# Linear attention into an RWKV channel mix on one core: another written-out order of the same pieces

## The chip, the core and the metric

The kernel runs on one core of one Trainium2 chip. The metric is the device time of one execution in microseconds (us); for the kernel before it is the median of three runs. The core has TensorE (PE in the profile; PEld is its weight load), VectorE (DVE), ScalarE (ACT), GpSimd (POOL) and SyncE (SP). Each works through its own list of instructions in the order in which the program gave them, and waits on semaphores for the others. POOL and SP issue DMAs here. The profile calls the queue of POOL's DMAs q0 (software_dynamic) and that of SP's DMAs q1 (hardware_dynamic); the packets of both go through the core's 16 DMA engines.

## The reference

The program computes attention without a softmax, normalizes each head by its root mean square, and feeds the result to a channel mix:

```python
kv = np.einsum('bhsd,bhse->bhde', k, v)          # q, k, v: 8 batches, 8 heads, 576 rows, 64 columns
out = np.einsum('bhsd,bhde->bhse', q, kv)
x = out / sqrt(mean(out*out, axis=-1) + 1e-6) * g_norm   # heads side by side: (8, 576, 512)

x_prev = x shifted down by one row, zeros first
xk = mu_k * x + (1 - mu_k) * x_prev
xr = mu_r * x + (1 - mu_r) * x_prev
k = relu(xk @ w_k)                               # 512 -> 1024
v = (k * k) @ w_v                                # 1024 -> 512
r = sigmoid(xr @ w_r)                            # 512 -> 512
return r * v                                     # float32
```

Inputs and output are float32; the kernel works in bfloat16 with float32 sums. The inputs are 28.3 MB of q, k and v and 5.2 MB of weights; the output is 9.4 MB.

## The kernel before

The work has two halves. The **attention** runs over 8 batches b. The **mix** runs over 9 groups g of 512 rows of all batches laid end to end, so a group needs the x of one or two batches: group 0 needs batch 0, group g batches g-1 and g, and group 8 batch 7.

Every step is a named *piece*, a function that issues a few instructions. `Plan.add` records a piece with the engines that it may run on and the pieces that it needs; `Plan.emit` (L95) goes through the string ORDER (L15) word by word and issues each piece. `@A` or `@D` behind a name puts it on ScalarE or VectorE where it may run on either. So ORDER alone sets the order on every engine and every DMA queue. The framework adds the semaphores that data and buffers need.

The pieces, by the first letters of their names (b is a batch, z a half of four heads, g a group):

- `ld.kB.z`, `ld.vB.z`, `ld.qB.z`, `ld.wk`, `ld.wr`, `ld.wv`: loads, issued on POOL (L272, L277, L292), converting to bfloat16. At most eight are in flight: each waits for the one eight before it.
- `z:512` (L478): a matmul on zeros, with no use but to keep TensorE busy. 35 of them, the last at 15.8 us.
- `kv` (L305), `kc` (copy, L182 or L184), `ks` (a split by a permutation, L311), `kd` (copy back): the 64x64 state of each head. `tq` (L390): q transposed on VectorE. `u` (L321): q times state, one PSUM tile for each half of the heads.
- `uc` (L188 on ScalarE, L190 on VectorE): a copy of u to SBUF, scaled by g. `sq` (L411, ScalarE): the square of u. Both read the same PSUM tile, and the framework lets the one that comes later in ORDER wait for the other.
- `ss` (L420, L436): sums of squares by a matmul. `rs` (L326, ScalarE): one over the root. From batch 2 on the factor comes out for each head once, into the single buffer `rsc`, and `sp` (L458) spreads it over the partitions by four DMAs on SP for each half. The next `rs` waits until both `sp` before it have landed.
- `mul` (L433, VectorE): u times the factor, that is x. `d` (L338): x minus the row before. `mk`, `mr` (L188 or L190): d times a column of mu. `xk`, `xr` (L351): the inputs of the mix.
- `k` (L510 for group 0, L534): xk @ w_k, two pieces for each PSUM tile; `relu` (L493, ScalarE); `ksq` (L521, L544, VectorE): the square. `r` (L556), `sig` (L566, ScalarE). `v` (L576), in two halves of the 1024 inner columns: `v2.3.0` is group 2, rows 384 to 511, first half.
- `out` (L589, L603, VectorE): sig times v; `out2.1` is for the rows of `v2.2.*` and `v2.3.*`. `st` (L484): the store of 128 rows, 256 KB, issued on SP.

`rs` needs another function table on ScalarE than `sig`; going from one to the other costs an ACT_TABLE_LOAD (L198). PSUM has four tiles of two banks for all of `kv`, `u`, `ss`, `k`, `r` and `v`; a piece that opens a tile waits until the readers of an earlier one are done. The buffers that matter below: three of k, v and q, three of `out` (each for two stores), three of `rs`, one `rsc`.

Of the kernel before, what the change touches and what calls it, by code (L numbers as in the profile page):

```python
# [19 lines left out]
d0.01 z:512 z:512 ks0.1 kd0.1@A z:512 u0.1.0 sq0.10 k0.000 uc0.10@A mk0.01@D xk0.01 u0.1.1 uc0.11@D sq0.11  # L20
ss0.10 k0.010 ss0.11 ld.wv0 ld.wv1 rs0.10 mul0.10 k0.110 d0.10 rs0.11 mk0.10@D xk0.10
mr0.00@A mul0.11 d0.11 mr0.10@A k0.011 relu0.01 xr0.10 mk0.11@D xk0.11 mr0.11@A k0.001 k0.100
mr0.01@D xr0.01 relu0.00 k0.111 xr0.00 relu0.11 k0.101 ld.v2.01 ksq0.01 xr0.11 relu0.10 ksq0.00
ld.k2.01 r0.0 tq1.01.1 r0.2 r0.3 sig0.1 r0.1 tq1.01.0 ksq0.10 ksq0.11 sig0.0 kv1.01
kc1.01@A ks1.01 kd1.01@A u1.01.1 uc1.11@D sq1.11 sq1.01 u1.01.0 uc1.10@D sq1.00 sq1.10 uc1.01@D
v0.1.0 v0.0.0 ss1.2 ss1.3 uc1.00@D ss1.0 v0.0.1 rs1.2 rs1.3 mul1.1 d1.1 rs1.0
ss1.1 rs1.1 mul1.0 d1.0 mk1.0@D v0.1.1 mk1.1@A v0.2.0 v0.2.1 xk1.1 mr1.1@A v0.3.0
v0.3.1 xk1.0 kv2.01 k1.4 k1.5 ld.q2.01 mr1.0@A kc2.01@A out0.0 ks2.01 kd2.01@A k1.2
tq2.01.1 relu1.2 k1.3 tq2.01.0 u2.01.1 out0.1 uc2.01@D relu1.1 k1.0 sq2.01 ld.v3.01 u2.01.0
sq2.11 sq2.00 sq2.10 uc2.11@D ld.k3.01 uc2.10@D k1.1 uc2.00@D ksq1.1 xr1.1 kv3.01 ss2  # L30
xr1.0 ld.q3.01 tq3.01.1 k1.6 k1.7 rs2 sp2.1 kc3.01@A ks3.01 r1.0 ld.q4.01 r1.1
# [19 lines left out]
v3.2.0 v3.2.1 ksq4.0 u7.01.1 mul5.0 sq7.01 ss6 mul5.1 st2.2 st2.1 rs6 uc7.01@D
sp6.0 d5.0 mr5.0@D v3.3.0 v3.3.1 ksq4.1 out3.1 r4.2 r4.3 sq7.11 v4.3.0 uc7.11@A
v4.3.1 sig4.1 u7.01.0 uc7.00@A st3.2 sq7.00 d5.1 mr5.1@A st2.0 v4.2.0 sp6.1 v4.2.1
mk5.1@D mk5.0@D v4.0.0 v4.0.1 xk5.1 xk5.0 out4.1 st4.2 xr5.0 k5.0 k5.6 st3.3
sq7.10 mul6.0 d6.0 uc7.10@A v4.1.0 ss7 mk6.0@D xk6.0 k5.1 k5.7 rs7 v4.1.1
k5.4 k5.5 relu5.3 mul6.1 relu5.0 k5.2 sp7.0 d6.1 st3.0 relu5.2 mr6.1@A xr5.1
mk6.1@D xk6.1 k6.6 mr6.0@D xr6.0 ksq5.0 k5.3 relu5.1 xr6.1 sp7.1 k6.2 ksq5.1
mul7.0 k6.3 relu6.1 k6.7 ksq6.1 relu6.3 k6.0 k6.1 r6.2 r6.3 d7.0 k6.4
k6.5 sig6.1 ksq5.3 relu6.2 ksq5.2 relu6.0 ksq6.0 ksq6.3 ksq6.2 r4.0 r4.1 v5.0.0
v5.0.1 mk7.0@D r6.0 v5.1.0 sig4.0 out4.0 r6.1 st4.0 sig6.0 v6.2.0 v6.2.1 mul7.1  # L60
v6.3.0 v6.3.1 d7.1 mr7.1@A st4.1 v6.1.0 xr7.1 mk7.1@A out6.1 st6.2 mr7.0@A xr7.0
r5.2 v6.0.0 v6.0.1 r5.3 r5.0 r5.1 xk7.0 sig5.1 sig5.0 xk7.1 v5.1.1 out5.0
st5.0 st5.1 st4.3 st6.3 k7.0 k7.6 k7.7 relu7.3 k7.2 k7.3 v6.1.1 k7.1
relu7.0 ksq7.3 v5.3.0 relu7.1 ksq7.1 v5.3.1 r8.2 out6.0 ksq7.0 k8.2 k8.3 v5.2.0
r8.3 relu8.1 st6.1 v5.2.1 ksq8.1 sig8.1 k7.4 k7.5 relu7.2 v7.1.0 ksq7.2 k8.6
k8.7 relu8.3 r7.2 r7.3 v7.2.0 v7.1.1 sig7.1 k8.0 out5.1 st5.2 ksq8.3 k8.1
r7.0 relu8.0 ksq8.0 r7.1 sig7.0 v7.3.0 k8.4 st6.0 v7.3.1 v7.0.0 v7.0.1 out7.0
st7.0 v7.2.1 out7.1 st7.3 st7.2 v8.1.00 k8.5 relu8.2 st7.1 ksq8.2 r8.0 st5.3
r8.1 sig8.0 v8.0.00 v8.1.10 v8.0.10 out8.00 st8.00 out8.10 st8.10 v8.2.00 v8.2.10 out8.20
# [575 lines left out]
```

## Time and profile before

| | |
|---|---|
| median of three runs | 208.15 us (207.28 to 208.63) |
| the profiled execution, its own time | 206.6 us |
| its span in the profile | 204.8 us |
| TensorE busy | 190.8 us, 1761 matmuls |
| VectorE busy | 136.6 us |
| ScalarE busy | 128.6 us, 10 table loads of 1.28 |
| DMA | 30.04 MB; loads (q0) 16.78 MB, spreads and stores (q1) 12.86 MB |

The times in the sections below count from the start of the span. The profile's part 2 cuts the span into 40 slices of 5.1 us and gives for each the busy share in tenths; matmuls are pipelined, so a busy TensorE is not a TensorE at its peak. In a row of the chain or the timeline the first number is the start and the second the length; in a row of the waits the numbers are the total, the count and the longest; in a row of the stretches the pairs are the engines' busy time and counts, and then come the granted clock of TensorE, the busy share of the DMA engines and GB/s.

From the trace one also sees the packets of each queue. The loads leave q0 in the order of their issue, without a pause until 96.4 us. The packets of the spreads and stores leave q1 in order as well:

| SP's DMA | issued (first, last) | packets, last end |
|---|---|---|
| sp2.1, sp2.0 | 54.05, 59.27 | 65.50 |
| st0.0, st0.2, st0.1 | 59.96, 61.04 | 67.38, 69.13, 71.91 |
| sp3.0, sp3.1 | 67.47, 72.36 | 79.73 |
| st1.3, st1.2 | 73.69, 74.07 | 81.94, 84.91 |
| sp4.1 | 82.69, 85.00 | 89.77 |
| st0.3 | 85.64 | 91.30 |
| sp4.0 | 86.32, 88.20 | 94.91 |
| st1.1, st2.3, st1.0 | 88.84, 93.46 | 95.21, 96.29, 97.84 |
| sp5.0, sp5.1 | 107.08, 112.38 | 114.14 |

### The profile page before, as it was taken

To read this page: it belongs to the slowest core of one execution; us is meant where nothing else is said; L and a number is where in the kernel's file an instruction comes from. 1 tells how busy PE (TensorE), PEld (TensorE's weight loads), DVE (VectorE), ACT (ScalarE), POOL (GpSimd) and SP (SyncE) were. 2 spreads that over 40 slices of the span, in tenths; PEclk is the share of its full clock that TensorE was granted. 3 is DMA by queue.
4 is the path that set the end of the run, shared out by engine and by line. 5 is a ranking of instruction groups with operands and counts; after the bars stand their busy time and mean duration, and the time that the engine had idled before them with its cause. 6 is when DMAs were issued, how large, how long until landed. Compare 5 with 4: busy or idle time off the path is not lost.

```text
span 204.8 us, 4262 instructions
## 1 busy us (share of the span) xinstructions
PE 190.8 (93%) x1761; PEld 94.0 (46%) x1761; DVE 136.6 (67%) x224; ACT 128.6 (63%) x171; POOL 24.5 (12%) x43
## 2 busy tenths in 40 slices
PE   7988895998899799998999999999999999999992
...
DMA  5999999999999999999003525360021051020254
GB/s 81 178 207 217 201 207 206 216 204 217 206 227 248 257 245 239 232 253 266 10 0 87 186 54 169 110 153 11 2 102 51 0 205 54 0 102 0 103 198 163
DMA packets 21015, 30.04 MB, mean 147 GB/s; under 512 B 1916, under 2 KB 14980, under 8 KB 20996
## 3 DMA queue, kind: packets, MB, share of 16 engines
q0 software_dynamic: 11808, 16.78, 46.2%
q1 hardware_dynamic: 9044, 12.86, 19.8%
...
## 4 chain that ended last, share of the span: by engine, by line
PE 61%; DVE 12%; ACT 9%; DMA 7%; SPq 5%; issue 3%; ACTq 0%; DVEq 0%
PE ps L534 20%; PE ps L576 18%; PE ps L556 13%; SPq L458 5%; DMA out_dram<-out 4%; PE ps L478 4%; DMA rs<-rsc 3%; ACT sq L411 3%; PE ps L510 3%; DVE uT L190 2%; DVE qT L390 2%; PE ps L321 2%; DVE out L589 2%; ACT rs L326 2%; PE ps L305 1%
## 5 line engine op out<-in xcount | busy, mean ns | idle before, releaser
L576 PE MATMUL ps<-w_v,sqk 128*128 128x512 bf16 (+1 forms) x296 | 67.1, 373 | 1.4 <-ACT sq L411 1.4
L534 PE MATMUL ps<-xk,w_k 128*128 128x512 bf16 (+1 forms) x288 | 59.2, 356 | 2.4 <-DVE xk L351 1.6
L493 ACT ACTIVATE relu<-ps 128x1024 bf16<-128x1024 f32 x36 | 36.1, 1024 | 30.9 <-PE ps L534 28.3
L576 PEld LDWEIGHTS <-sqk 128*128 128x128 bf16 x296 | 28.5, 98 | 33.7 <-issue 2.8
L534 PEld LDWEIGHTS <-w_k 128*128 128x128 bf16 x288 | 27.5, 98 | 29.5 <-issue 2.6
L544 DVE TENSOR_TENSOR sqk<-relu 128x1024 bf16<-128x1024 bf16 x32 | 21.4, 685 | 22.3 <-ACT relu L493 15.9
L556 PE MATMUL ps<-w_r,xr 128*128 128x512 bf16 x144 | 34.4, 379 | 0.0
L589 DVE TENSOR_TENSOR out<-ps,sig 128x1024 f32<-128x1024 f32 x16 | 19.4, 1220 | 11.2 <-PE ps L576 4.6
L566 ACT ACTIVATE sig<-ps 128x1024 bf16<-128x1024 f32 x18 | 18.2, 1025 | 10.3 <-PE ps L556 10.1
L411 ACT ACTIVATE sq<-ps 128x576 bf16<-128x576 f32 (+2 forms) x32 | 19.7, 651 | 7.5 <-DVE uT L190 4.8
L390 DVE STREAM_TRANSPOSE qT<-q 128x576 f32<-128x576 f32 (+1 forms) x18 | 20.7, 1192 | 4.3 <-DMA q<-in_q_dram 4.2
L188 ACT ACTIVATE md<-d,cols 128x576 bf16<-128x576 bf16 (+2 forms) x32 | 20.9, 720 | 0.5 <-DVE d L338 0.5
L556 PEld LDWEIGHTS <-xr 128*128 128x128 bf16 x144 | 13.6, 98 | 16.3 <-issue 0.9
L190 DVE TENSOR_SCALAR uT<-ps,cols 128x576 bf16<-128x576 f32 (+2 forms) x16 | 12.7, 815 | 10.2 <-ACT sq L411 7.0
L433 DVE TENSOR_TENSOR xT<-uT,rs 128x1152 bf16<-128x1152 bf16 (+2 forms) x18 | 12.3, 687 | 5.3 <-ACT rs L326 3.6
L351 DVE TENSOR_TENSOR xr<-md,xT 128x1152 bf16<-128x1152 bf16 (+2 forms) x18 | 12.1, 687 | 3.2 <-ACT md L188 3.1
L198 ACT ACT_TABLE_LOAD x10 | 12.8, 1283 | 0.9 <-PEq L629 0.7
L338 DVE TENSOR_TENSOR d<-xT 128x1152 bf16<-128x1152 bf16 (+2 forms) x18 | 12.4, 689 | 0.5
L190 DVE TENSOR_SCALAR md<-d,cols 128x576 bf16<-128x576 bf16 (+2 forms) x40 | 12.3, 351 | 0.5
L188 ACT ACTIVATE uT<-ps,cols 128x576 bf16<-128x576 f32 (+2 forms) x16 | 11.7, 744 | 1.1 <-PE ps L321 1.1
L351 DVE TENSOR_TENSOR xk<-md,xT 128x1152 bf16<-128x1152 bf16 (+2 forms) x18 | 12.0, 687 | 0.2
L478 PE MATMUL ps<-zero 128*128 128x512 bf16 x35 | 10.5, 448 | 1.2 <-DVE ident L219 1.2
...
## 6 DMA issues: line engine op xcount, KB each, us to landing
...
k<-in_k_dram POOLq DMA_DIRECT2D x4, 288.0 KB, 12.4
...
```

The source lines that it names most:

```text
L188: nc.scalar.mul(out=dst, in_=src, mul=col)
L190: nc.vector.tensor_scalar(out=dst, in0=src, scalar1=col, scalar2=None, op0=ALU.mult)
L351: nc.vector.tensor_tensor(out=dst[:, 2 * z:2 * z + 2, r0:r0 + w], in0=md.t[:, :, cs], in1=xT[:, :, cur], op=ALU.add)
L390: nc.vector.transpose(out=dst[part, js, :], in_=src[part, js, :])
L411: sq_ = add("sq" + name, "A", lambda _, ps=ps, sq=sq, cs=cs, w=w: nc.scalar.activation(out=get(sq)[:, :, cs], in_=ps.t[:, :, 0:w], func=AF ...
L478: nc.tensor.matmul(get(k_ps[(0, 0)])[:, 0, 0:n], zero[:, 0:128], zero[:, 0:n], start=not started, stop=not started)
L493: nc.scalar.activation(out=get(rt), in_=ps.t, func=AF.Relu)
L534: nc.tensor.matmul(get(ps)[:, fc % 2, a0:a1], w_k_sb[:, cc, 128 * fc:128 * fc + 128], xk[:, cc, x0:x0 + a1 - a0], start=(cc == 0), stop=(c ...
L544: nc.vector.tensor_mul(out=get(sqk)[:, 2 * f2:2 * f2 + 2, :], in0=rt.t, in1=rt.t)
L556: nc.tensor.matmul(get(ps)[:, ci % 2, :], xr[:, cc, n0:n0 + 128], w_r_sb[:, cc, :], start=(cc == 0), stop=(cc == NHP - 1))
L576: nc.tensor.matmul(get(ps)[:, bank, cs], sqk.t[:, fc, 128 * ci:128 * ci + 128], w_v_sb[:, fc, cs], start=(fc == 0), stop=(fc == NFC - 1))
L589: dv = add(f"out{g}.{c2}", "D", lambda _, ps=ps, sg=sg, ot=ot: nc.vector.tensor_mul(out=get(ot), in0=ps.t, in1=sg.t), deps=ms + [sg_done], ...
```

## The change

Only ORDER is changed: the sequence of its words, and the engine of some pieces that may run on two. The pieces, their instructions and their buffers are the same, and so are the 35 zero matmuls; 26 of them (`zz` and 25 more) now stand ahead of `kv0.0`, where it was 28. The new order comes out of a search over the order and the engines of all pieces, in which the readers of one PSUM tile go in turn, the copies and stores of one queue go in turn, and the loads are lengthened by both.

Of the pieces that may run on two engines, 43 are now on ScalarE and 43 on VectorE; it was 45 and 41. ScalarE goes between the tables of `rs` and `sig` so that it loads a table 12 times instead of 10. The diff, cut to the front, to batches 2 to 4 with groups 1 to 4, and to the end:

```diff
-table ld.q0.0 ld.v0.0 ld.k0.0 small ld.q0.1 ld.v0.1 ld.k0.1 ld.wk0 ld.v1.0 ld.wk1 seta
-zz z:512 z:512 z:512 z:512 z:512 z:512 z:512 z:512 z:512 z:512 z:512 z:512 z:512 z:512 z:512 z:512 z:512 z:512 z:512 z:512 z:512 z:512 z:512 z:512 z:512 z:512 z:512 kv0.0 tq0.0.1 tq0.0.0 kc0.0@A ident tr9 setb cols ld.q1.01 perm ks0.0
-tq0.1.0 tq0.1.1 ld.wr kd0.0@A z:512 u0.0.0 sq0.00 u0.0.1 sq0.01 z:512 ss0.00 rs0.00 z:512 z:512 ss0.01 uc0.00@D
-mul0.00 uc0.01@A ld.k1.1 d0.00 mk0.00@D ld.k1.0 ld.v1.1 xk0.00 rs0.01 kv0.1 mul0.01 kc0.1@A
...
-kd3.01@D tq3.01.0 relu1.0 ksq1.0 relu1.3 ksq1.3 sig1.0 r1.2 u3.01.0 tq4.01.1 sp2.0 r1.3
-v1.2.0 uc3.10@A v1.3.0 st0.0 sq3.10 st0.2 v1.0.0 sig1.1 sq3.00 uc3.00@D u3.01.1 sq3.11
-st0.1 sq3.01 v1.1.0 uc3.01@A uc3.11@A ld.k4.01 ksq1.2 v1.0.1 v1.3.1 ld.v4.01 kv4.01 mul2.1
-d2.1 mk2.1@D ss3 mul2.0 d2.0 mk2.0@D xk2.1 rs3 sp3.0 v1.1.1 v1.2.1 xk2.0
-ld.k5.01 out1.0 kc4.01@A ks4.01 ld.q7.01 tq4.01.0 kd4.01@D k2.4 k2.5 ld.k7.01 mr2.0@A mr2.1@A
-relu2.2 out1.1 xr2.0 ksq2.2 ld.v5.01 k2.2 k2.3 relu2.1 u4.01.0 sq4.00 sp3.1 uc4.10@A
-st1.3 st1.2 k2.6 sq4.10 uc4.00@D k2.7 xr2.1 ksq2.1 ld.q5.01 mul3.0 d3.0 k2.0
-relu2.3 k2.1 relu2.0 mk3.0@D ksq2.0 u4.01.1 uc4.01@A sq4.01 r2.2 r2.3 sq4.11 mul3.1
-ld.q6.01 ld.k6.01 r2.0 ksq2.3 kv5.01 uc4.11@A kc5.01@D ss4 rs4 sp4.1 sig2.1 tq5.01.1
-r2.1 sig2.0 ks5.01 kd5.01@A v2.0.0 v2.0.1 st0.3 v2.1.0 v2.1.1 mr3.0@A v2.3.0 d3.1
-mk3.1@D xk3.1 tq5.01.0 u5.01.1 sq5.01 uc5.11@A uc5.01@A sq5.11 mr3.1@A tq7.01.0 sp4.0 v2.2.0
...
-r3.0 r3.1 tq6.01.0 sig3.0 kv6.01 kv7.01 ksq3.3 kc6.01@A mk4.1@D ss5 kc7.01@D r3.2
-d4.0 mk4.0@D ks6.01 st2.3 r3.3 st1.0 kd6.01@A v3.1.0 v3.1.1 xk4.1 ks7.01 v3.0.0
-sig3.1 v3.0.1 kd7.01@D u6.01.1 xk4.0 rs5 mr4.0@A sq6.01 sq6.11 out3.0 xr4.0 sp5.0
-uc6.01@A uc6.11@D tq7.01.1 k4.6 sp5.1 k4.7 relu4.3 k4.4 k4.0 k4.1 relu4.0 k4.5
...
-v8.3.01 v8.3.11 out8.31 st8.31 v8.3.00 v8.3.10 st8.20 out8.30 st8.30
+table ld.q0.0 ld.v0.0 small ld.k0.0 ld.q0.1 ld.v0.1 ld.k0.1 seta zz z:512 z:512 z:512 z:512 z:512 z:512 z:512 z:512 z:512 z:512 z:512 z:512 z:512 z:512 z:512 z:512 z:512 z:512 z:512 z:512 z:512 z:512 z:512 z:512 z:512 kv0.0 setb
+perm tq0.0.0 ident tr9 tq0.0.1 tq0.1.1 cols kc0.0@A ks0.0 kd0.0@A z:512 u0.0.1 sq0.01
+z:512 u0.0.0 sq0.00 uc0.01@D tq0.1.0 uc0.00@A ld.wk0 z:512 z:512 ss0.00 rs0.00 kv0.1 kc0.1@A ss0.01 ks0.1
+kd0.1@A z:512 u0.1.1 rs0.01 sq0.11 ld.k1.1 ld.v1.0 ld.wk1 uc0.11@A u0.1.0 sq0.10 ld.wr z:512 z:512 ss0.11
...
+k1.7 relu1.3 ld.k3.01 u2.01.0 sq2.10 uc2.00@D k1.4 sq2.00 k1.5 u2.01.1 uc2.10@D relu1.2
+xr1.1 sq2.01 xr1.0 uc2.01@D v1.1.0 v1.0.0 sq2.11 ss2 kv3.01 uc2.11@D rs2 sp2.0
+r1.0 ksq1.3 r1.1 ksq1.2 v1.1.1 kc3.01@A tq3.01.1 tq3.01.0 ld.q4.01 ks3.01 sig1.0 sp2.1
+ld.k4.01 kd3.01@A v1.0.1 out1.0 u3.01.1 uc3.11@A sq3.11 ld.v4.01 uc3.01@A r1.2 r1.3 ld.q5.01
+v1.3.0 v1.3.1 sig1.1 kv4.01 sq3.01 u3.01.0 kc4.01@A st0.0 sq3.00 sq3.10 uc3.00@A mul2.0
+d2.0 mk2.0@D xk2.0 ld.v5.01 v1.2.0 ks4.01 kd4.01@A v1.2.1 mul2.1 uc3.10@A ss3 d2.1
+mk2.1@D rs3 sp3.0 xk2.1 mr2.1@D mr2.0@A out1.1 xr2.1 sp3.1 k2.2 k2.6 k2.7
+k2.3 relu2.1 tq4.01.0 relu2.3 tq4.01.1 ld.k5.01 ksq2.1 xr2.0 k2.0 k2.1 tq5.01.0 relu2.0
+ksq2.0 st0.2 mul3.0 ld.k6.01 st1.2 k2.4 u4.01.0 ld.q7.01 k2.5 tq5.01.1 uc4.10@A relu2.2
+r2.0 ksq2.3 r2.1 st1.0 sq4.10 r2.2 r2.3 mul3.1 v2.2.0 sq4.00 st0.3 ksq2.2
+sig2.1 v2.3.0 kv5.01 sig2.0 uc4.00@D d3.0 mk3.0@D u4.01.1 uc4.01@A kc5.01@A d3.1 v2.2.1
+ld.v6.01 v2.3.1 sq4.01 ks5.01 mk3.1@D uc4.11@A st1.1 v2.0.0 v2.0.1 kd5.01@A out2.1 u5.01.1
+xk3.0 mr3.0@D xk3.1 sq4.11 ss4 rs4 sp4.0 uc5.11@A v2.1.0 uc5.01@D v2.1.1 out2.0
+st2.0 k3.0 xr3.0 sq5.11 k3.1 sq5.01 relu3.0 k3.2 u5.01.0 mr3.1@D uc5.00@A k3.3
+sq5.00 xr3.1 ld.q6.01 k3.4 k3.5 r3.0 r3.1 mul4.0 d4.0 mk4.0@D ksq3.0 sq5.10
+uc5.10@A relu3.2 ksq3.2 sig3.0 ld.v7.01 xk4.0 sp4.1 mul4.1 k3.6 k3.7 relu3.3 d4.1
+mk4.1@D relu3.1 r3.2 r3.3 xk4.1 sig3.1 st2.3 kv6.01 ss5 mr4.0@D kc6.01@D k4.0
+k4.1 k4.6 rs5 sp5.0 k4.7 sp5.1 ksq3.1 relu4.0 ld.k7.01 tq6.01.0 tq6.01.1 ks6.01
...
+st7.3 r8.3 st8.10 v8.0.00 v8.2.00 sig8.1 v8.0.10 st7.1 out8.00 v8.2.10 out8.20 st8.20
+st8.00 v8.3.00 v8.3.01 v8.3.11 out8.31 st8.31 v8.3.10 out8.30 st8.30
```

More of the change, by code (lines that the diff above doesn't have):

```diff
@@ L20 @@
[L20 to L31, printed above, removed]
@@ L38 @@
-st1.3 st1.2 k2.6 sq4.10 uc4.00@D k2.7 xr2.1 ksq2.1 ld.q5.01 mul3.0 d3.0 k2.0
-relu2.3 k2.1 relu2.0 mk3.0@D ksq2.0 u4.01.1 uc4.01@A sq4.01 r2.2 r2.3 sq4.11 mul3.1
-ld.q6.01 ld.k6.01 r2.0 ksq2.3 kv5.01 uc4.11@A kc5.01@D ss4 rs4 sp4.1 sig2.1 tq5.01.1
-r2.1 sig2.0 ks5.01 kd5.01@A v2.0.0 v2.0.1 st0.3 v2.1.0 v2.1.1 mr3.0@A v2.3.0 d3.1
-mk3.1@D xk3.1 tq5.01.0 u5.01.1 sq5.01 uc5.11@A uc5.01@A sq5.11 mr3.1@A tq7.01.0 sp4.0 v2.2.0
-v2.3.1 out2.0 xk3.0 v2.2.1 out2.1 k3.4 k3.5 mul4.1 xr3.0 xr3.1 u5.01.0 tq6.01.1
@@ L44 @@
-relu3.2 ld.v7.01 st1.1 uc5.00@A mul4.0 k3.2 k3.3 relu3.1 ksq3.1 d4.1 mr4.1@D xr4.1
-sq5.00 k3.6 k3.7 sq5.10 ksq3.2 uc5.10@A ld.v6.01 k3.0 k3.1 relu3.0 ksq3.0 relu3.3
-r3.0 r3.1 tq6.01.0 sig3.0 kv6.01 kv7.01 ksq3.3 kc6.01@A mk4.1@D ss5 kc7.01@D r3.2
-d4.0 mk4.0@D ks6.01 st2.3 r3.3 st1.0 kd6.01@A v3.1.0 v3.1.1 xk4.1 ks7.01 v3.0.0
-sig3.1 v3.0.1 kd7.01@D u6.01.1 xk4.0 rs5 mr4.0@A sq6.01 sq6.11 out3.0 xr4.0 sp5.0
-uc6.01@A uc6.11@D tq7.01.1 k4.6 sp5.1 k4.7 relu4.3 k4.4 k4.0 k4.1 relu4.0 k4.5
-u6.01.0 relu4.2 k4.2 k4.3 sq6.00 ksq4.3 uc6.00@D uc6.10@D ksq4.2 st3.1 sq6.10 relu4.1
@@ L51 @@
[L51 to L69, printed above, removed]
-v8.3.01 v8.3.11 out8.31 st8.31 v8.3.00 v8.3.10 st8.20 out8.30 st8.30
+table ld.q0.0 ld.v0.0 small ld.k0.0 ld.q0.1 ld.v0.1 ld.k0.1 seta zz z:512 z:512 z:512 z:512 z:512 z:512 z:512 z:512 z:512 z:512 z:512 z:512 z:512 z:512 z:512 z:512 z:512 z:512 z:512 z:512 z:512 z:512 z:512 z:512 z:512 kv0.0 setb
@@ new lines @@
+perm tq0.0.0 ident tr9 tq0.0.1 tq0.1.1 cols kc0.0@A ks0.0 kd0.0@A z:512 u0.0.1 sq0.01
+z:512 u0.0.0 sq0.00 uc0.01@D tq0.1.0 uc0.00@A ld.wk0 z:512 z:512 ss0.00 rs0.00 kv0.1 kc0.1@A ss0.01 ks0.1
+kd0.1@A z:512 u0.1.1 rs0.01 sq0.11 ld.k1.1 ld.v1.0 ld.wk1 uc0.11@A u0.1.0 sq0.10 ld.wr z:512 z:512 ss0.11
+ld.v1.1 rs0.11 mul0.00 ld.q1.01 d0.00 mr0.00@D mk0.00@D z:512 z:512 ss0.10 ld.k1.0 xk0.00 k0.010 rs0.10
+xr0.00 ld.wv0 k0.000 mul0.01 d0.01 mk0.01@D xk0.01 k0.110 mr0.01@D xr0.01 uc0.10@A mul0.10
+d0.10 mk0.10@D xk0.10 k0.100 k0.001 relu0.00 ld.wv1 k0.011 relu0.01 mul0.11 d0.11 mk0.11@D
@@ new lines @@
+xk0.11 k0.101 relu0.10 mr0.10@D xr0.10 ksq0.00 r0.0 r0.1 sig0.0 k0.111 relu0.11 mr0.11@D
+xr0.11 r0.2 r0.3 tq1.01.0 tq1.01.1 sig0.1 ksq0.11 ksq0.10 ksq0.01 ld.k2.01 kv1.01 kc1.01@A
+ks1.01 kd1.01@A u1.01.1 sq1.11 uc1.11@D ld.v2.01 sq1.01 uc1.01@D u1.01.0 sq1.10 v0.0.0 uc1.10@D
+sq1.00 ss1.0 rs1.0 v0.0.1 ss1.1 ld.q2.01 uc1.00@D v0.1.0 rs1.1 ld.v3.01 ld.q3.01 mul1.0
+d1.0 ss1.3 rs1.3 ss1.2 rs1.2 mul1.1 d1.1 mk1.0@A v0.2.0 mk1.1@D v0.2.1 xk1.0
+xk1.1 v0.3.0 v0.3.1 out0.1 mr1.0@A kv2.01 kc2.01@A v0.1.1 ks2.01 k1.2 out0.0 k1.3
@@ new lines @@
+tq2.01.0 mr1.1@A relu1.1 k1.0 st0.1 tq2.01.1 ksq1.1 kd2.01@A k1.1 relu1.0 ksq1.0 k1.6
+k1.7 relu1.3 ld.k3.01 u2.01.0 sq2.10 uc2.00@D k1.4 sq2.00 k1.5 u2.01.1 uc2.10@D relu1.2
[3 more added lines that the diff above has]
+v1.3.0 v1.3.1 sig1.1 kv4.01 sq3.01 u3.01.0 kc4.01@A st0.0 sq3.00 sq3.10 uc3.00@A mul2.0
@@ new lines @@
+kd6.01@A tq7.01.1 relu4.3 v3.2.0 st1.3 ksq3.3 u6.01.0 sq6.10 sq6.00 uc6.00@A st2.1 v3.3.0
+v3.3.1 mr4.1@D uc6.10@D v3.2.1 xr4.1 u6.01.1 uc6.01@A uc6.11@A sq6.01 mul5.0 d5.0 mr5.0@D
+v3.1.0 v3.1.1 out3.1 v3.0.0 k4.2 ksq4.0 sq6.11 k4.3 relu4.1 k4.4 mul5.1 d5.1
+mk5.1@D xr4.0 kv7.01 kc7.01@D ksq4.1 ss6 rs6 k4.5 sp6.0 tq7.01.0 ks7.01 v3.0.1
+r4.2 out3.0 st3.1 mr5.1@A xr5.1 kd7.01@D relu4.2 ksq4.2 r4.3 v4.2.0 mk5.0@D u7.01.1
+v4.3.0 ksq4.3 sig4.1 xk5.0 uc7.11@A xk5.1 v4.1.0 sq7.01 uc7.01@A v4.3.1 mul6.0 d6.0
@@ new lines @@
+st3.2 mk6.0@D v4.2.1 sq7.11 k5.2 k5.3 k5.6 relu5.1 k5.7 relu5.3 k5.4 st3.0
+out4.1 k5.5 xk6.0 relu5.2 st2.2 sp6.1 mul6.1 v4.0.0 v4.0.1 d6.1 st4.3 ksq5.2
+mk6.1@A xk6.1 u7.01.0 sq7.00 uc7.00@D r4.0 v4.1.1 uc7.10@D r4.1 sig4.0 out4.0 k5.0
+k5.1 sq7.10 mr6.0@A k6.4 k6.5 relu6.2 k6.6 mr6.1@D ksq5.3 relu5.0 st4.1 st4.2
+k6.2 k6.7 ksq6.2 relu6.3 k6.3 ksq5.1 st3.3 ksq5.0 v5.2.0 v5.3.0 ss7 st4.0
+rs7 k6.0 k6.1 relu6.0 v5.0.0 ksq6.3 v5.3.1 sp7.0 relu6.1 v5.2.1 ksq6.1 xr5.0
+mul7.0 d7.0 v5.1.0 v5.1.1 ksq6.0 v5.0.1 xr6.0 sp7.1 r5.0 r5.1 sig5.0 r5.2
```

8 lines of the change are left out of this document (added).

## The prediction

> **What bounds the kernel now.** I read the page's parts 1 to 3, then the engines' busy time in stretches of 5 us, then TensorE's matmuls in order of time, the waits, the chain that ended last, and the packets of the two DMA queues. Busy time and slices:
>
> ```profile
> PE 190.8 (93%) x1761; PEld 94.0 (46%) x1761; DVE 136.6 (67%) x224; ACT 128.6 (63%) x171; POOL 24.5 (12%) x43
> ...
> PE   7988895998899799998999999999999999999992
> ...
> DMA  5999999999999999999003525360021051020254
> ```
>
> TensorE is the bound, but not evenly. Laid along ORDER, its matmuls follow each other without a gap (216 ns for one of 512 columns) from about 118 us to 200.95 us. What it loses lies before: of 200.95 us, 11.4 are the 35 matmuls on zeros and some 12 are gaps, nearly all before 95 us. Until there the DMA engines are saturated (nines in the third row, to 96.4 us, when the last load's packets end), so the first half is paced by chains of waits on busy queues. A new order can win only from those gaps, and loses when it opens others. Two stretches of the chain show what such gaps are made of:
>
> ```profile
> 59.27 6.91 DMA rs<-rsc
> ...
> 66.30 0.77 DVE xT L433
> 67.10 0.77 DVE d L338
> 67.89 0.65 DVE md L190 x2
> ...
> 69.93 3.63 PE ps L534 x16
> ...
> 85.64 6.09 DMA out_dram<-out
> ...
> 91.83 1.23 DVE out L589
> ```
>
> The first is the spread of batch 2 (sp2): its last DMA takes 6.91 us to land among the loads, then mul, d, mk and xk run on VectorE, then k2. The second is store st0.3: issued at 85.64, landed at 91.73, and only then may VectorE write that out buffer again. The waits show that it stood for it:
>
> ```profile
> DVE out L589 <- DMA out_dram<-out: 2.5, 1, 2.5
> DVE xT L433 <- DMA rs<-rsc: 1.6, 2, 1.2
> ```
>
> **The change part by part.** Every piece is kept, so TensorE's 1761 matmuls are the same. I compare the moment at which the changed order has done a given amount of TensorE work with the moment at which the old one had done as much.
>
> *Front, to k1.* Two zero matmuls fewer stand before kv0.0: 2 x 0.216 = 0.43 us, so kv0.0 starts at 8.87 instead of 9.30 (the packets of ld.k0.0 end at 8.24, no new wait). From there I add durations along the chain kc, ks, kd, u, sq, ss, rs, mul, d, mk, xk with their rows (0.37, 0.31, 0.37, 0.25 to 0.41, 0.60 to 0.70, 0.25, 0.69 to 0.80, 0.45, 0.45, 0.5, 0.45): kv1.01 comes at 29.75 (was 30.20), its four loads having landed by 28.7 in both orders since they are the same bytes in one saturated queue. On POOL perm (0.82) and ident (0.19) now precede ld.wk0, whose packets start only at 12.4 in either order; ld.wk1 has one half load more ahead of it (1.5) and lands near 20.6 instead of 18.97, and k0.001 asks for it at 22.3. Both cost nothing while the queue ahead of them is that long. After kv1 the normalizers of half 0 go first: the table load starts at 35.1 (was 36.22), mul1.0 at 37.8 (38.92), k1 at 43.1 (44.02). **Gain 1.0 us.**
>
> *k1 to k2.* The gain is lost again: rs2 needs all four sq2 pieces, and these stand on ScalarE behind relu1.0, 1.3 and 1.2 (1.02 each). I get rs2 at 53.3 to 54.0; the row has 53.28. Store st0.1 stands ahead of sp2.0 now, but is issued at 45.4 and has landed by 54. So the eight DMAs of sp2 are issued from 54.1 and the last lands at 66.2 as before. What follows is shorter by one xk (0.6 us): mul2.1 0.80, d 0.80, mk 0.7, xk 0.75 from 66.4 give **k2 at 69.5 (was 69.93): gain 0.45.** By then TensorE has done everything else; it finishes ss3 at 65.4 and stands for **4.1 us**. In the old order that hole was 1.3 us:
>
> ```profile
> 68.27 0.39 PE L311 MATMUL ps<-kvn,perm 128*128 128x128 bf16 x4
> 69.93 3.63 PE L534 MATMUL ps<-xk,w_k 128*128 128x512 bf16 x16 [1.28 <-DVE xk L351]
> ```
>
> *The stores of groups 0 and 1.* Here the change costs. On SP, st0.2 st1.2 st1.0 st0.3 st1.1 now stand in a row behind sp3 and are issued from 73.3 to 76.0; before, only st1.3 and st1.2 were (73.69, 74.07), the others at 85.6 and later. The queue's packets leave in order: sp3's last ended at 79.73, the first store's began at 77.50. Beside loads of q a store takes 3.06 us (st0.0, 64.32 to 67.38) and beside loads of k or v 1.83 (st0.2, 67.30 to 69.13); the bounds are 1.3 (st1.1) and 4.4 (st1.3). With the new loads q7, v6, q6, v7 in the load queue's slots 77 to 91 I take 3.6, 1.8, 3.5, 1.8: st0.3 ends at 88.1 and its signal comes 0.5 later (91.30 to 91.83 before). out2.1 writes the buffer of st0.2 and st0.3; its matmuls are done at 85.2, so VectorE waits 3.4 us, to 88.7. The old wait of 2.5 us hid behind four k3 pieces. The new one does not: ss4 needs out2.1's PSUM buffer, and out2.1 stands on VectorE ahead of xk3.0, mr3.0 and xk3.1, which k3 needs. ss4 starts at 90.05 instead of 87.7, and k3 at 92.2, where the old order had done as much at 90.30. **Loss 2.35; balance +1.9.**
>
> *Batch 4.* rs4 now follows ss4 at 90.5 (the old rsc of batch 4 ran at 81.92) with a table load that it did not need before; the load (1.28) ends at 88.5, hidden by the wait for out2.1, and would cost 1.3 without it. sp4.0 goes out from 91.25; with the 4.8 to 5.8 us of the rows it lands near 98. Then VectorE has ten pieces in a row to xk4.1 (mul, d, mk, two ksq, xk, mul, d, mk, xk: 7.15 us): k4 at 105.1. TensorE is there at 104.2. The old order had this work done at 102.87: **+2.2**. Before, v3, kv7 and k4 were parted so that this chain lay beside other work.
>
> *From there.* After 98 us a spread DMA lands in 1.75 us and stores in 1.6 to 2.2. The chains of batches 5 to 7 then fit: sp5 from 107.3 as before, v3.3.1 and u7.01.1 wait 0.2 and 0.45; the old u7.01.1 lost 0.64. From k5 on TensorE is full in both. Two switches of ScalarE's table more than before (12 against 10, 1.28 each) lie at rs4 and sig3.0, beside matmuls. In the tail st8.00 stands between the last stores: 0.2. **Sum: +2.2 + 0.2 = +2.4**: a span of 207.2, 209.0 us beside the profiled 206.6. The median of the three runs, 208.15, is 1.55 above that profile; put on it, **210.5 us**.
>
> *A hole and the clock.* At the span's end the last matmul ends at 200.95, and the clock falls 2.2 us later:
>
> ```profile
> 202.00:203.00 1.00, 0.00 (x0) 0.00 (x0) 0.00 (x0) 0.00 (x0) 0.00 (x0) 1.00 0.39 131
> 203.00:204.00 1.00, 0.00 (x0) 0.00 (x0) 0.00 (x0) 0.00 (x0) 0.00 (x0) 0.59 0.00 0
> ```
>
> The cold start shows the price of getting it back: the zero matmuls follow each other by 0.43 us from 1.19 until about 5.2 and by 0.216 after, so 4.0 us at half speed, 2.0 us lost. A hole of 4.1 us before k2 is longer than those 2.2, so I take it that the clock may fall. I cost it at nothing: TensorE has 2.35 us to spare before ss4, where it waits for out2.1. Without that wait it costs 2.0. The Trainium skill, "TensorE: Matmul & The Clock Gate", section "HAM oscillation — how this bites in real kernels", warns of gaps over about 3.4 us and has the next burst start at half rate; by it the hole before k2 is the change's weak point. The trace agrees that an idle TensorE loses its clock (2.2 us after the last matmul); no gap within the old run is long enough to test it.
>
> **The rivals.** That the order is not carried out can be left out: every engine's list of instructions follows ORDER as written.
> 1. *The lead is kept: faster.* Place: rs2. If ScalarE reaches rs2 as early as k1 is (1.0 us), sp2 and k2 follow at 68.9, and if stores take 1.6 each (the row of st0.3), st0.3 ends at 83.8 and out2.1 waits for nothing; if then sp4.0, issued at 88.3, lands in 4.7 us, k4 has no stall either. -1.0, and the old stalls at u5.01.0 (0.59) and u7.01.1 (0.64) gone: -2.2, **206.0**. It decides when st0.3 has landed before 85. For it: 1.0 us is in hand at k1. Against it: the q loads beside the stores, and 4.8 to 5.8 us in every loaded spread row.
> 2. *The stores land in time, batch 4 does not.* Without the wait, rs4 ends at 89.3, sp4.0 lands at 96.5, k4 comes at 103.7: +0.8, with the tail +1.0, **209.2**. If the clock also falls, the 2.0 us have no cover, and it is the forecast's time again by another way.
> 3. *The queue is worse.* All four stores at the 4.4 us of the slowest row: st0.3 ends at 95.0, but the loads ending at 96 speed up the last; at a mean of 3.7 it ends at 92.2, 4.1 later than I take, of which batch 4 gets nothing back while its spreads get faster by 3 us (4.8 to 1.75): +3.5 in all, **211.6**; with the clock's 2.0 lost beside it, 213.6. For it: st1.3 and st1.2 took 7.4 us together. Against it: only two of the four stand beside q loads.
>
> **How the numbers follow.** Forecast (store wait, then batch 4; 210.5, from 209.3 to 211.5 as the stores take 2.2 to 3.0): 0.45. Rival 1: 0.18. Rival 2: 0.20. Rival 3: 0.17. The runs shown spread by 0.65%, so 1% (206.1 and 210.2) is about what can be told from no change. Of the forecast two thirds lie above 210.2; with rival 3 slower has 0.47. Rival 1 lies mostly below 206.1: faster 0.15. The rest, rival 2 with the lower part of the forecast: within 1%, 0.38. The range goes from rival 1's edge to rival 3's: 206.3 to 213.4. The forecast and rival 3 alone would be 209.3 to 213.6.
>
> **What the profile of the changed kernel will show.** Right, if k1 starts near 43 and k2 near 69.5 after a hole of about 4 us; if VectorE has a wait of 3 us or more for out_dram<-out ahead of an out piece near 86 to 89, with TensorE waiting at ss4 for VectorE; if k4 starts near 105 with xk4.1 just ended; and if TensorE is full from about 130. Wrong, if that wait is under 1 us (rival 2), if rs2 ends by 53 (rival 1), if sp4.0 lands before 95, or if matmuls of 512 columns run at 0.43 us after a hole and nothing later absorbs it. The weakest numbers are the time of a store beside loads, seen in nine cases only, and my adding of durations on ScalarE from 43 to 54 us, where one piece more or less in the way is 0.7 us.

## The result and the profile after

The changed kernel takes **209.69 us** (208.67 to 211.61), the kernel before, in the same comparison, 207.77 (206.96 to 208.63). The ratio is 1.0104, with a 95% interval from 1.0074 to 1.0135: 1.9 us slower. The forecast was 210.5.

The profiled execution of the changed kernel is the slowest of its runs, 211.61 us with a span of 209.8. Its page, busy time and slices:

```profile
PE 193.6 (92%) x1761; PEld 95.6 (46%) x1761; DVE 139.1 (66%) x232; ACT 127.2 (61%) x165; POOL 24.5 (12%) x43
...
PE   7589998699999599969999999999999999999991
...
PEclk9955699999999999999999999999999999999999
DMA  5999999999999999995304318205040441000254
```

PEclk is the granted clock in tenths. Two things are to be seen. TensorE has low slices at 68 to 73 us (5 tenths; the lowest of before there was 7) and at 89 to 94 us (6), where the DMA engines are still at nine tenths, and nothing but nines between 95 us and the last slice. And the clock was at half from 10.89 to 24.55 us: in this execution the last of ld.k0.0's signals came at 11.25 us (8.77 before), after the zero matmuls had ended near 8.2. Eight of the 13 runs have a mean clock as low as 0.959 to 0.973, so this execution was not alone in it; but these eight are no slower than the other five (median 209.5 us against 210.3). An experiment below shows too that the front is not what the median pays.

The chain of the changed kernel, in order of time, in place of the two stretches shown of before:

```profile
74.55 6.96 DMA rs<-rsc
81.53 10.67 DMA out_dram<-out
...
92.39 1.23 DVE out L589
...
93.66 0.43 PE ps L420 x8
```

The last DMA of sp3.0 takes 6.96 us. Store st0.3 is issued at 81.53 and lands 10.67 us later; only then does VectorE run out2.1, and only then TensorE ss4. The waits of the same execution (total, count, longest):

```profile
DVE xT L433 <- DMA rs<-rsc: 4.2, 3, 3.7
...
DVE out L589 <- DMA out_dram<-out: 3.5, 2, 3.2
...
PE ps L534 <- DVE xk L351: 3.0, 2, 2.3
...
PE ps L420 <- DVE out L589: 1.8, 1, 1.8
```

VectorE's wait for the spreads was 1.6 before; TensorE's wait at ss4 did not exist. And TensorE in order of time, at the hole ahead of k2:

```profile
69.81 0.43 PE L420 MATMUL ps<-sq,heads 128*32 128x288 bf16 x8
70.88 0.60 PE L534 MATMUL ps<-xk,w_k 128*128 128x512 bf16 x2 [0.64 <-DVE xk L351]
73.82 5.77 PE L534 MATMUL ps<-xk,w_k 128*128 128x512 bf16 x26 [2.33 <-DVE xk L351]
```

To compare kernels I add up what TensorE loses: from the start of one piece to the start of the next, less the time of the piece back to back (0.216 us for a matmul of 512 columns). Zero matmuls count as lost, and so does half clock. In us, by stretch of the span, of the profiled executions that are compared below:

| kernel | 0-45 | 45-60 | 60-75 | 75-95 | 95-end | sum |
|---|---|---|---|---|---|---|
| before | 17.3 | 2.3 | 2.2 | 0.9 | 0.9 | 23.6 |
| changed | 21.0 | 0.4 | 3.5 | 2.6 | 0.5 | 28.0 |
| a_z8 | 17.9 | 0.4 | 5.9 | 1.3 | 0.5 | 26.0 |
| a_st | 18.8 | 0.6 | 5.5 | 0.7 | 0.5 | 26.1 |
| f_k2 | 18.0 | 0.4 | 4.1 | 4.5 | 0.5 | 27.5 |
| f_all | 17.6 | 0.4 | 4.2 | 3.2 | 1.1 | 26.5 |
| f_st2r | 17.6 | 0.4 | 4.5 | 2.6 | 1.1 | 26.2 |
| a_nold | 18.6 | 0.4 | 1.3 | 0.0 | 0.4 | 20.8 |
| b_nold | 17.7 | 2.3 | 0.7 | 0.3 | 0.9 | 21.9 |

The new order wins 1.9 us between 45 and 60 and 0.4 at the end. It loses between 60 and 95 us. The table compares single executions: that of before took 1.2 us less than its median, that of the changed kernel 1.9 more than its own and that of a_st 1.3 more, so its columns tell more than its sums. Where a piece lies at the edge of two stretches, a few tenths can go to either.

### The profile page after: what moved, and what is told of

It is laid out like the page before. It is cut to its first block, busy times and chain, and to the rows that moved or that the text cites. A ratio compares the mean times of both kernels' runs of the same rounds, so it can differ in the third digit from the quotient of the medians.

```text
span 209.8 us, 4241 instructions
## 1 busy us (share of the span) xinstructions
PE 193.6 (92%) x1761; PEld 95.6 (46%) x1761; DVE 139.1 (66%) x232; ACT 127.2 (61%) x165; POOL 24.5 (12%) x43
## 4 chain that ended last, share of the span: by engine, by line
PE 78%; DMA 13%; ACT 3%; DVE 1%; issue 1%; SPq 1%; POOL 1%; ACTq 0%; DVEq 0%; POOLq 0%
PE ps L576 27%; PE ps L534 23%; PE ps L556 13%; DMA out_dram<-out 5%; DMA k<-in_k_dram 4%; PE ps L510 4%; DMA rs<-rsc 3%; PE ps L321 3%; PE ps L305 3%; PE ps L478 2%; PE ps L436 1%; PE ps L311 1%; PE ps L420 1%; ACT sq L411 1%; SPq L458 1%
## 5 line engine op out<-in xcount | busy, mean ns | idle before, releaser
L576 PE MATMUL ps<-w_v,sqk 128*128 128x512 bf16 (+1 forms) x296 | 67.8, 374 | 1.4 <-DVE uT L190 1.4
L534 PE MATMUL ps<-xk,w_k 128*128 128x512 bf16 (+1 forms) x288 | 58.0, 356 | 3.0 <-DVE xk L351 3.0
L190 DVE TENSOR_SCALAR md<-d,cols 128x576 bf16<-128x576 bf16 (+2 forms) x52 | 15.8, 353 | 0.5
L188 ACT ACTIVATE uT<-ps,cols 128x576 bf16<-128x576 f32 (+2 forms) x18 | 13.2, 740 | 3.9 <-PE ps L321 3.9
L190 DVE TENSOR_SCALAR uT<-ps,cols 128x576 bf16<-128x576 f32 (+1 forms) x14 | 11.0, 818 | 5.1 <-ACT sq L411 4.6
L188 ACT ACTIVATE md<-d,cols 128x576 bf16<-128x576 bf16 x20 | 14.2, 765 | 0.1
L478 PE MATMUL ps<-zero 128*128 128x512 bf16 x35 | 12.1, 489 | 1.2 <-DVE zero L218 1.2
```

Of the source, the lines that this page charges most:

```text
L188: nc.scalar.mul(out=dst, in_=src, mul=col)
L190: nc.vector.tensor_scalar(out=dst, in0=src, scalar1=col, scalar2=None, op0=ALU.mult)
L534: nc.tensor.matmul(get(ps)[:, fc % 2, a0:a1], w_k_sb[:, cc, 128 * fc:128 * fc + 128], xk[:, cc, x0:x0 + a1 - a0], start=(cc == 0), stop=(c ...
L576: nc.tensor.matmul(get(ps)[:, bank, cs], sqk.t[:, fc, 128 * ci:128 * ci + 128], w_v_sb[:, fc, cs], start=(fc == 0), stop=(fc == NFC - 1))
```

## The experiments

Theories: **F**, the front costs it (fewer zeros ahead of kv0.0); **S**, the wait for the store does; **C**, the clock that falls in the holes does; **D**, the new order's own waits between engines do; **E**, formed on the way, the transfers that run beside the loads do. Line numbers in the experiments' profiles differ from those above by up to six.

### Front and stores

*a_z8*: eight zero matmuls more ahead of kv0.0.

```diff
-z:512 kv0.0 setb
+z:512 z:512 z:512 z:512 z:512 z:512 z:512 z:512 z:512 kv0.0 setb
```

> The changed kernel with 8 more zero matmuls ahead of kv0.0 (34 instead of 26). Theory F (front): the changed order's zeros end at 8.2 us while the last of ld.k0.0's 16 signals came at 11.25 in its profile; the hole lets the clock fall to half (10.89 to 24.55 us), and that is where the time goes. Then these zeros keep the clock: mean granted clock back from 0.965 to 0.99 or more, kv1.01 near 31 instead of 34.8, time 207.5 to 208.3 against 209.7. Theory S (stores): the wait of out2.1 for store st0.3 sets k3 whatever the front does; then the clock comes back and the time stays at 209.3 to 210.3, with a larger wait of TensorE at ss4.

Measured: 209.66, ratio 1.0083 [1.0054, 1.0111]. The front runs at full clock (the clock falls once, at 71.39 us) and the time is that of the changed kernel, as S foretold: **F falls.** S also foretold a larger wait at ss4; it got smaller, as the waits of this profile show:

```profile
DVE out L583 <- DMA out_dram<-out: 3.5, 2, 3.0
...
PE ps L414 <- DVE out L583: 1.0, 1, 1.0
```

and its engines around the hole ahead of k2 (busy time and counts of PE, PEld, DVE, ACT, POOL; then the granted clock, the DMA share and GB/s):

```profile
66.50:71.40 4.90, 1.09 (x11) 0.33 (x11) 4.73 (x10) 4.17 (x6) 0.00 (x0) 1.00 1.19 235
71.40:74.80 3.40, 3.34 (x8) 1.17 (x8) 3.40 (x7) 0.00 (x0) 0.00 (x0) 0.50 1.21 228
```

In 4.9 us TensorE works 1.09, and for the next 3.4 us it has half its clock.

*a_st*: st0.2 and st0.3 right behind st0.1, ahead of the spreads of batch 2.

```diff
-k1.0 st0.1 tq2.01.1
+k1.0 st0.1 st0.2 st0.3 tq2.01.1
...
-ksq2.0 st0.2 mul3.0
+ksq2.0 mul3.0
...
-sq4.00 st0.3 ksq2.2
+sq4.00 ksq2.2
```

> The changed kernel with st0.2 and st0.3 moved forward on SP, right behind st0.1 and ahead of the spreads of batch 2; the front is left. Theory S: out2.1 no longer waits (3.2 us on VectorE in the profile), ss4 follows u5.01.1 at once, and the time falls by 1.5 to 2.3, to about 207.7. Theory F: the clock stays near 0.97 and the time at 209.2 to 210, since what is lost in front is lost; the two stores in front of sp2 may even cost up to 0.5.

*a_z8st*: both edits.

> Both edits. If the two causes lie one behind the other and each hides part of the other, neither alone gives all and both together give the most: 206.0 to 207.0, below the kernel before (207.8). F alone: as with the zeros alone. S alone: as with the stores alone.

Measured: 208.55, ratio 1.0040 [1.0021, 1.0059], and 208.88, ratio 1.0043 [1.0018, 1.0067]. The wait ahead of ss4 is gone in both profiles. **S holds for 1.1 us** of the 1.9 (1.3 by the ratios, 0.8 between a_z8 and a_z8st); the intervals of the changed kernel and of a_st are apart. That is less than the 1.5 to 2.3 that S foretold, and both edits together missed their 206.0 to 207.0 by 2 us. What is left is not the front.

*b_zm2*: the kernel before with two zero matmuls fewer ahead of kv0.0, the count of the changed order.

> The kernel before with two zero matmuls fewer ahead of kv0.0 (26, as in the changed order). F: the hole that this opens loses the clock there too in most executions: mean clock under 0.985, time up by 1 to 3 us, 209 to 211. If two zeros don't matter and the changed order's front is slow for another reason (readers in turn, the order of kc, uc, sq): time within 0.5 of 207.8 and the clock at 0.99.

Measured: 207.88, ratio 0.9988 [0.9952, 1.0023]. The two zeros alone change nothing that can be told, although in the profiled execution (209.07) kv0.0 waited 1.3 us and the clock fell at 11.13 us for 6.83.

### Keeping the clock

The runs list a mean granted clock. One stretch of 3.41 us at half clock is 0.0083 of it. The changed kernel's runs have 0.959 to 0.984, those of before mostly 0.99 to 1.00. So zeros were put into the holes, each into the PSUM tile of the piece that follows:

```diff
+            if word.startswith("y:"):
+                _, name, n = word.split(":")
+                for _ in range(int(n)):
+                    fill(self.pieces[name])
...
+    def fill(p):
+        buf = next(x for x in p.bufs if x.tag == "ps")
+        nc.tensor.matmul(get(buf)[:, 0, 0:512], zero[:, 0:128], zero[:, 0:512], start=True, stop=True)
...
-uc3.10@A ss3 d2.1
+uc3.10@A y:ss3:6 ss3 d2.1
...
-sp3.1 k2.2 k2.6
+sp3.1 y:k2.2:9 k2.2 k2.6
```

> The changed kernel with fifteen 512-column matmuls of zeros more in the hole of TensorE ahead of mix group 2: six ahead of ss3, nine ahead of k2.2, each into a PSUM tile that the next piece overwrites. Theory C (the loss that the stores do not explain is the clock that falls in that hole): no half-clock stretch between 69 and 78 us, granted clock up by about 0.008 (one stretch of 3.41 us), and of the 1.7 us that such a stretch costs the part that the wait for st0.3 does not cover, so 0.3 to 0.9 us off the time: 208.8 to 209.4. The wait for st0.3 ahead of ss4 stays or grows. Theory D (the clock is a symptom, the order itself is late): unchanged, 209.7, or later by what the zeros hold up.

*f_all* adds `y:kv1.01:2`, `y:u1.01.1:3` ahead of ks1.01, `y:u1.01.1:2` and `y:u1.01.0:5`; *f_st2* is f_all with the stores of a_st; *f_before* has the zeros around kv1.01 in the old order.

> The changed kernel, its stores where it has them, with the zero matmuls in both late holes. Theory C: the wait for st0.3 is now alone, uncovered by half-clock time, so that it costs more than the 1.1 us seen with the clock down: the kernel stands 1.2 to 2.2 us above the one with stores moved and the same zeros, at 208.3 to 209.2. Theory D: 209.7 less nothing, and 1.1 above that one.

> The changed kernel with st0.2 and st0.3 right behind st0.1, and with zero matmuls in both late holes of TensorE: twelve around kv1.01, ks1.01 and the two u1.01 pieces, fifteen ahead of ss3 and k2.2. With the stores moved alone it took 208.55 at a granted clock of 0.98. Theory C: the clock is 0.99 or more, and what then remains of the new order is no later than the kernel before: 206.8 to 207.5. Theory D: 208.3 to 208.7, whatever the clock.

> The kernel before with the twelve zero matmuls around kv1.01, ks1.01 and the two u1.01 pieces, the hole that both kernels have. Its clock is 0.99 to 1.0 in nearly all runs, so there is little to win: theory C 207.3 to 207.8, at a clock of 0.997 or more and with less spread. Were the zeros themselves worth something in another way, or in the way, it would show here: below 207.0 or above 208.2.

| | us | ratio | clock of the runs |
|---|---|---|---|
| f_k2 | 210.75 | 1.0122 [1.0058, 1.0185] | 0.974 to 0.982 |
| f_all | 210.91 | 1.0138 [1.0069, 1.0207] | 0.981 to 0.995 |
| f_st2 | 208.99 (nine runs) | 1.0061 [1.0020, 1.0102] | 0.972 to 1.00 |
| f_before | 208.09 | 1.0000 [0.9961, 1.0039] | 0.992 to 1.00 |

f_st2's profiled execution took 511.84 us, with TensorE slow throughout; it is left out, and f_st2 is read from the times of its nine other runs. The zeros made no kernel faster: f_k2 and f_all stand no better than the changed kernel, f_st2 no better than a_st, f_before where before stands, and the times that C foretold for f_k2 (208.8 to 209.4), f_st2 (206.8 to 207.5) and f_all (208.3 to 209.2) were all missed. That f_all takes 1.9 us more than f_st2 fits S, but their intervals overlap. In f_k2 the clock held in the hole ahead of k2, but fell at 34.25 us and at 92.28, the second time 0.75 us after the wait ahead of ss4 had ended. In f_all the clock is full from 4.5 us to the end, and the profile stands no better than a_z8's. Its waits between 60 and 95 us say why:

```profile
DVE xT L432 <- DMA rs<-rsc: 4.7, 3, 4.1
DVE out L592 <- DMA out_dram<-out: 4.2, 1, 4.2
...
PE ps L419 <- DVE out L592: 2.6, 1, 2.6
```

TensorE comes to ss4 2 us earlier than in a_z8 and waits 2.6 us instead of 1.0: st0.3's packets end at 88.47, against 88.66. **C falls as a cause of its own:** what the clock loses ahead of k2 is lost in front of a store that comes no sooner.

Part of that store's wait is not its data. A DMA has landed when the last of its 16 signals is there. For st0.3 the fifteenth came at 89.07 in a_z8 and the last at 90.18, with out2.1 starting at 90.37; in f_all it was 88.84 and 89.83, in f_k2 89.20 and 90.07. In the profile of before the two lay 0.07 apart. So 0.9 to 1.1 us of this wait, in a_z8 as much as TensorE waits at ss4, hung on one late signal. What delays it, the runs don't tell.

### What is left without the stores and at full clock

*f_st2r* is f_st2 once more. *a_late* puts st0.3 one place further back.

```diff
-sq4.00 st0.3 ksq2.2
+sq4.00 ksq2.2
...
-uc4.11@A st1.1 v2.0.0
+uc4.11@A st1.1 st0.3 v2.0.0
```

> Once more the changed kernel with st0.2 and st0.3 right behind st0.1 and with the zero matmuls in both late holes: the first time its runs lay between 207.62 and 210.71 and its profiled execution was disturbed. Theory S and C together (stores and clock make up the whole loss): clock 0.99 or more in most runs, no wait ahead of ss4, 206.8 to 207.9, at or below the kernel before. Theory D (the new order is late by itself): 208.3 to 209.5, with a clock of 0.99 or more, and then the profile shows the place, a wait of TensorE that neither a store nor the clock explains.

> The changed kernel with st0.3 one place further back on SyncE, behind st1.1 instead of ahead of it; nothing else. Theory S (from 80 us on the transfers of SyncE land one after the other, and out2.1 and ss4 wait for the place that st0.3 has in that row): st0.3 now lands where st1.1 landed, 2.65 to 3.16 us later by the two profiles that show both, and all of it reaches the end, since nothing is left ahead of ss4 to take it up: 211.9 to 212.9. Theory C (the lost clock is what costs, the wait for the store only stands in time that would be lost anyway): 209.4 to 210.2.

f_st2r: 209.31, ratio 1.0060 [1.0034, 1.0086], clock 0.99 or more in nine of twelve runs: neither store nor clock, and still late, as D foretold. TensorE and VectorE of it, in order of time:

```profile
81.83 1.89 PE L579 MATMUL ps<-w_v,sqk 128*128 128x512 bf16 x8
85.67 0.77 PE L304 MATMUL ps<-v,k 64*64 64x64 bf16 x72 [1.94 <-DVE uT L189]
```

```profile
83.52 0.76 DVE L432 TENSOR_TENSOR xT<-uT,rs 128x1152 bf16<-128x1152 bf16 x1 [1.79 <-DMA rs<-rsc]
84.20 0.68 DVE L547 TENSOR_TENSOR sqk<-relu 128x1024 bf16<-128x1024 bf16 x1
84.80 0.81 DVE L189 TENSOR_SCALAR uT<-ps,cols 128x576 bf16<-128x576 f32 x1
```

In this execution a third transfer has come to the front. mul3.1 waits for the spread sp3.1, whose packets end at 81.44; behind it on VectorE stands uc4.00, the second reader of a PSUM tile that kv5.01 needs. TensorE stands 1.94 us. In a_z8 it comes to kv5.01 at 85.3 and does not wait. Here too a late signal has the larger part: of sp3.1's last DMA fifteen signals were there at 81.86, the last at 83.40, so that by these numbers some 1.5 us of the wait are that signal's. The same happened to st1.3 (114.71 and 116.27, with VectorE waiting 1.8 us for it), when no loads ran any more. So sp2.1 (k2), sp3.1 (kv5.01) and st0.3 (ss4) stand one behind the other, and theory E says that whoever takes one away meets the next; this profile alone does not show it.

a_late: 209.62, ratio 1.0073 [1.0038, 1.0109], not 211.9, and inside the range that C foretold. But the edit missed its aim. out2.1 starts at 89.97, when the last signal of st1.1 (89.85) is there and that of st0.3 (92.27) is not. So with the stores exchanged out2.1 has the buffer of st1.0 and st1.1, and waited for st1.1, now in st0.3's place:

```profile
89.97 1.23 DVE L583 TENSOR_TENSOR out<-ps,sig 128x1024 f32<-128x1024 f32 x1 [1.86 <-DMA out_dram<-out]
```

It says nothing for or against S or C, and shows that the order of stores also chooses the buffers.

### The loads taken away

*a_nold* and *b_nold* leave out the nine loads of batches 5 to 7 in both orders.

```diff
-    kvq = {(n, b): Buf(n) for n in "kvq" for b in range(B)}
+    kvq = {(n, b): Buf(n) for n in "kvq" for b in range(5)}
+    kvq.update({(n, b): kvq[(n, 4)] for n in "kvq" for b in range(5, B)})
...
         def fn(_):
+            if b >= 5:
+                return
```

> The changed kernel without the nine loads of batches 5 to 7: these batches read the tiles of batch 4, so the output of batches 5 to 7 is that of other inputs; every other instruction, wait and transfer stays. The loads then end near 60 us instead of near 95. Theory E (between 60 and 95 us TensorE is tied to transfers of SyncE that are slow because they run beside loads: sp2.1 ahead of k2.2, sp3.1 ahead of kv5.01 by way of mul3.1 and uc4.00, st0.3 ahead of ss4; taking one away only brings the next to the front, which is why zeros, moved stores and a later st0.3 moved the time so little): spreads and stores land within 1.8 us, the hole ahead of k2.2 shrinks from 4.1 us to under 1.5, the waits at kv5.01 and ss4 are gone, and the time falls by 3 to 5.5 us, to 204.2 to 206.7. Theory D (the order's own waits between engines hold TensorE): the hole and the time stay within 1 us, 208.7 to 210.

> The kernel before without the nine loads of batches 5 to 7, in the same way. Its TensorE lost 3.1 us between 60 and 95 us against 6.1 in the changed kernel, so there is less to win: 205 to 206.8. What counts is the difference of the two without these loads. Theory E: the changed order is then no later than the old one, from 1.5 us ahead to 0.3 behind, since it was 1.3 us ahead of it at 60 us in the runs without trouble at the front. Theory D: the changed order stays 1.4 us or more behind.

Measured: the changed order 204.32, ratio to before 0.9804 [0.9769, 0.9839]; the old order 205.33, ratio 0.9875 [0.9835, 0.9916]. Without these loads the changed order is **1.0 us ahead**; with them it is 1.9 behind. The two intervals meet at their edges, but five of the changed order's six runs are below the fastest of the old order's, and both times and their difference lie where E foretold. In a_nold the spreads of batch 3 land, issue to last packet, in 1.69 to 1.76 us (4.8 to 6.7 in the changed kernel), the five stores after them in 1.9 to 2.6 (6.4 to 11.0). The changed order first, with its loads:

```profile
60.00:75.00 15.00, 12.03 (x164) 5.50 (x163) 10.46 (x17) 11.94 (x18) 1.35 (x3) 1.00 1.16 230
75.00:95.00 20.00, 17.80 (x203) 8.17 (x201) 15.83 (x25) 14.08 (x19) 2.03 (x3) 1.00 1.07 236
```

and a_nold, without:

```profile
60.00:75.00 15.00, 13.76 (x183) 6.25 (x184) 13.08 (x20) 12.62 (x18) 0.00 (x0) 1.00 0.35 88
75.00:95.00 20.00, 19.63 (x217) 9.06 (x213) 17.88 (x30) 16.87 (x25) 0.00 (x0) 1.00 0.41 127
```

The DMA share falls from 1.16 to 0.35 and TensorE's loss from 60 to 95 us from 6.1 to 1.3, although every other wait of the order is still in the program. In the old order it falls from 3.1 to 1.0. **E holds, D falls.** It is not that work had waited for the loads that are left out: in the profiles of before, the changed kernel and a_z8 no wait for a load is listed from 60 us on. Nor do the engines run faster without them: a mul takes 0.75 us in a_nold and 0.76 in the changed kernel, a relu 1.02 in both. What the changed order adds to the slow transfers is where it puts them: sp2's packets end at 67.3 to 70.0 instead of 65.5, five stores follow sp3 in a row, and TensorE, 1.3 us ahead, is out of other work sooner. The hole ahead of k2 is the slow packets' doing: in a_st no last signal came more than 0.6 us after the fifteenth between 60 and 120 us, and its hole is 4.29 us. In the waits at kv5.01 and ss4 the late signals had a large part, as shown above. They are fewer without the loads (between 27 and 119 us none in a_nold, seven in f_all), so that these runs do not say how much of E is the one and how much the other. By which resource the loads slow the others, the 16 engines or the memory, no run here tells; the Trainium skill, "DMA: Bandwidth & Descriptors", section "Queues, rings and completion order", says that each engine takes turns between the queues that have work, packet by packet. The latencies above agree with that, and don't prove it.

## Why the prediction came out as it did

**The direction and the store wait were foreseen; that the sum came so near is in part luck.** It gave +2.4 us over the profile of before; in a_z8, the changed order without its trouble at the front, TensorE loses 26.0 us against 23.6 and the time after its last matmul is 0.4 longer: a span of 207.6, where 207.2 was said. On the medians it is +1.9. But the lead at k1 was missing and another came later, the stores' terms offset each other, and the stall of batch 4 never came. Putting the forecast on the median of three runs added 1.55; beside the changed kernel the median of before is 207.77, so 0.4 of the 0.8 that the forecast was too high is this.

*Front, to k1.* 1.0 us was said. At k1 it isn't there: at full clock (f_st2r) k1.2 starts at 44.5, not 43.1, because kv1.01 comes at 30.3 to 30.9 and not at 29.75. Of ld.k1.0, now the last load that kv1.01 needs, most signals are there at 28.6 to 29.7, but the last comes at 30.20 in a_st, 30.24 in f_k2 and 30.91 in f_all, and kv1.01 starts 0.04 to 0.05 later. In before it came at 28.23. The lead arises later, where the old order's stalls between 45 and 60 us (kv2, u2, kv3, ss2) are gone: 1.3 us at 60 us in a_z8 (17.28 + 2.30 lost before, 17.85 + 0.40 there).

*k1 to k2.* The hole of 4.1 us is right: TensorE idles 1.61 + 2.49 = 4.10 us in a_z8, 4.29 in a_st, 3.19 in the changed kernel's own profile. Its place is not: k2 runs in earnest from 71.1 to 73.8 us on, not 69.5. rs2 starts at 54.8 to 56.0 where the clock holds until 30 us (53.3 to 54.0 was said), and the last spread takes 6.6 to 6.9 us to its last packet, where it was 6.2 in before, and ends at 67.3 to 68.7. That the hole came out as said, though k2 was 1.5 us and more later, is luck: TensorE was later by about as much.

*The stores.* The mechanism and the size of VectorE's wait are as predicted: 3.2 us, and 3.0 in a_z8, against 3.4, with TensorE at ss4 behind it. Three terms of it were off, and two of them nearly cancelled: the row began 3 us later (80.6, as sp3 was later) and a store took 2.1 us (1.7, 2.2, 2.6, 1.9 in a_z8), not 2.7, so that st0.3's packets end at 88.66 where 88.1 was said. The third is its signal, 0.5 us behind the packets by the prediction: it came 1.3 to 1.5 behind in a_z8, f_k2 and f_all and 2.2 in the changed kernel. The loss of 2.35 at ss4 measured 1.0 and 1.8, and 2.5 to 2.6 where the clock was kept ahead of k2; taking the wait away won 1.1. The rest had been lost ahead of it already, and that is the step the prediction passed over: it had only one late transfer at a time.

*Batch 4.* **This step failed.** sp4.0 went out at 92.2 to 94.9, when the loads were ending, and its DMAs took 1.7 to 2.4 us to their last packets, not 4.8 to 5.8. k4 followed without a stall. Of the balance only 0.3 hung on it, since the stall was set against a later old order.

*A hole and the clock.* Costed at nothing because of the wait at ss4, and that is what f_k2 and f_all show: with the clock kept TensorE waits 2.6 us at ss4 instead of 1.0, and wins nothing. The clock did fall, in the hole ahead of k2, in the profiles of a_z8, a_st, a_z8st and a_late, for 3.41 us each. Where the stores were moved the cover was gone, but the kernels that kept the clock then (f_st2, f_st2r) were no faster than a_st, so the 2.0 of the prediction never showed. In the one profile of these the time went into sp3.1's wait, most of it a late signal.

*The rivals.* Rival 1's lead is real, 1.3 us, but was not kept. Rival 2, without the store wait, was put at 209.2; a_st, which has none, takes 208.55 with a clock of 0.965 to 0.992. Rival 3's slow stores were not seen.
